# Row maxima of two heads negated and split before their transposition, and sent by one transfer instead of four

## The chip, the cores and the metric

The kernel runs on one core of one Trainium2 chip. Its metric is device microseconds of one execution. TensorE multiplies matrices and transposes, VectorE, ScalarE and GpSimd work on the elements, and the queue of SyncE (SP) issues every transfer between memories in program order.

## The reference, cut to what matters

The reference is a transformer block: a layer norm with a modulation, causal attention in 4 segments of 512 tokens with a memory carried from segment to segment, an output projection, and then a mixer MLP over the tokens. The attention of one head and one segment is what the change touches:

```python
# S=2048 tokens, D=1024, 32 heads of 32, N=4 segments of L=512
logits = einsum("bhqd,bhkd->bhqk", qs, ks) * scale + mask
p      = softmax(logits, axis=-1)
a_dot  = einsum("bhqk,bhkd->bhqd", p, vs)
num, den = phi(qs) @ M, phi(qs) @ z + 1e-6
o = g * num/den + (1-g) * a_dot
M, z = M + phi(ks)^T @ vs, z + sum(phi(ks))
```

The softmax needs the maximum of each row of logits, which is taken off before the exponential.

## The kernel before, in words

All matrices run as 32-bit numbers split in two parts, a high part and a rest (`split`), and products are made of three terms. The attention stage goes over 32 steps `t`: 8 groups of 4 heads, 4 segments, two passes. One step projects keys, values and queries of 4 heads (`project`, lines 194 and 202), and each of its 4 heads then goes through three stages that the loop at the end of the attention interleaves: `maxima` (three heads ahead), `scores`, and `values` (one head behind). Work that is prepared for later steps (weights, modulation rows, reloads) is planned between them. The program is written in this order, and a planner then orders the instructions of each engine by the times that it reckons; each engine runs its own list strictly in that order.

For each head there is a stacked tile `sk` with 98 rows: `stack` (lines 332 to 334) copies the parts of queries and keys into rows 0 to 95 by three transfers, with the queries in the left 512 columns and the keys in the right. Rows 96 and 97 hold, under the keys, ones, and under the queries the negated row maximum in two parts. So the product of `scores` over 98 rows gives logits less their maximum at once, already transposed for the product with the values. Before that product can run, rows 96 and 97 must have come.

`maxima` makes them. Four products on the 96 rows (line 438) give the logits with queries as rows, and VectorE reduces each to a column of `mx` (line 439). Every second head, TensorE transposes the 8 columns of two heads (line 445, `nmps`, in the one bank named `ms`), ScalarE writes the negated high part (line 447), VectorE the rest (line 448), and SP issues four transfers, one for each head and part, that bring them from 4 rows of 128 to one row of 512 (line 452). `scores` starts at line 473. There are 64 such pairs of heads.

The tiles `sk` exist twice, for even and odd steps, with one tile for each head:

```python
skt = [[q.tile([98, 2, L], F32R, name=f"sk{i}_{h}") for h in range(4)] for i, q in enumerate(sk_)]
```

The transfers use eight completion semaphores in turn; a transfer waits until the one eight places before it has landed.

Of the kernel before, what the change touches and what calls it, by code (L numbers as in the profile page):

```python
# [7 lines left out]
F32 = mybir.dt.float32  # L8
F32R = mybir.dt.float32r
F16 = mybir.dt.float16  # L10
BF16 = mybir.dt.bfloat16
AF = mybir.ActivationFunctionType
ALU = mybir.AluOpType
# [5 lines left out]
P = 128  # L19
NSEG, L = 4, 512  # L20
# [25 lines left out]
def attention_and_mlp(ctx, tc, x, wq, wkv, wo, beta, w1, b1, w2, b2, c, wm_a, wm_b, out):  # L46
    nc = tc.nc
    V, A, G, T, SY = nc.vector, nc.scalar, nc.gpsimd, nc.tensor, nc.sync
# [17 lines left out]
    a = par.__enter__()  # L66
# [9 lines left out]
    def bank(tag, bufs, name):  # L76
        return psum.tile([P, 512], F32, tag=tag, bufs=bufs, name=name)

    A.preload_act_table_set("natural_log_exp_and_others")
    ident = top.tile([P, P], F32, name="ident")  # L80
# [176 lines left out]
    for i in range(2):  # L257
        ps = bank("pj", 2, f"scps{i}")
# [43 lines left out]
    b = late.__enter__()  # L302
    skp = [tc.tile_pool(name=f"sk{i}", bufs=1, reuse_waits="tile") for i in range(2)]
    sk_ = [q.__enter__() for q in reversed(skp)]
    sk_.reverse()
    skt = [[q.tile([98, 2, L], F32R, name=f"sk{i}_{h}") for h in range(4)] for i, q in enumerate(sk_)]
    for sk in skt[0] + skt[1]:
        G.memset(sk[96:98, 1].bitcast(F32), 1.0)
    for g in range(NG):
        G.tensor_tensor(bdg[:, g, 0:128].rearrange("p (h e) -> p h e", h=4),  # L310
                        bd[:, 0:128].rearrange("p (h e) -> p h e", h=4),
# [10 lines left out]
    st = {}  # L322
# [3 lines left out]
    def stack(t, h):  # L326


        sk = st[t]["sk", h] = skt[t % 2][h]
        skf = sk.bitcast(F32)  # L330
        src = st[t]["sg"].bitcast(F32)[32 * h:32 * h + 32]
        SY.dma_start(skf[0:32], src[:, 0:3:2])
        SY.dma_start(skf[32:64], src[:, 0:4:3])
        last_sk[t, h] = SY.dma_start(skf[64:96], src[:, 1:3])

    def project(t, piece):
# [28 lines left out]
        elif piece == 2:  # L365
# [26 lines left out]
            for h in range(3):  # L392
                stack(t, h)
        else:
            stack(t, 3)
            vp, r1 = d["vp"], d["r1"]
            A.copy(vp[:, :, :, 33:65], r1)
# [28 lines left out]
                G.tensor_tensor(MZ[:, g], MZ[:, g], tm, op=ALU.add)  # L426

    def maxima(t, h):
        d = st[t]
        if h % 2 == 0:  # L430
            d["mx"] = b.tile([P, 2, 4], F32, tag="mx", bufs=2, name=f"mx{t}_{h}")
        mx = d["mx"]
        q, k = d["sk", h][0:96, 0], d["sk", h][0:96, 1]
        x = bank("s1", 2, f"sx_{t}_{h}")
        y = bank("s1", 2, f"sy_{t}_{h}")
        z = bank("s1", 2, f"sz_{t}_{h}")
        for i, o in ((0, x[:, 0:128]), (2, x[:, 128:512]), (1, y[:, 0:256]), (3, z)):
            T.matmul(o, q[:, 128 * i:128 * i + 128], k[:, 0:128 * i + 128], start=True, stop=True)  # L438
            marks[4 * t + h - LEADS, "V"] = V.tensor_tensor_reduce(  # L439
                o, o, mask[:, 384 - 128 * i:], 1.0, -3.0e38, op0=ALU.add, op1=ALU.max,  # L440
                accum_out=mx[:, h % 2, i:i + 1])
        if h % 2 == 0:
            return
        ps = bank("ms", 1, f"nmps{t}_{h}")
        T.transpose(ps[0:8, 0:128], mx.rearrange("p a b -> p (a b)"), ident)
        nt = [b.tile([8, P], F32R, tag=f"nt{i}", bufs=2, name=f"nt{i}_{t}_{h}") for i in range(2)]
        A.activation(nt[0], ps[0:8, 0:128], AF.Copy, scale=-1.0)
        V.scalar_tensor_tensor(nt[1], ps[0:8, 0:128], -1.0, nt[0].bitcast(F32), op0=ALU.mult, op1=ALU.subtract)
        for hh in range(2):
            sk = d["sk", h - 1 + hh]  # L450
            for part in range(2):
                SY.dma_start(sk[96 + part:97 + part, 0].bitcast(F32).rearrange("p (b n) -> p b n", n=128),
                             nt[part][4 * hh:4 * hh + 4].bitcast(F32))

    marks = {}

# [156 lines left out]
    for g in range(2, NG):  # L613
        n = 8 * g - 13
# [5 lines left out]
    for j in range(32):  # L620
        n = ML0 + MLS * j
        later(n, lambda j=j: mod_fetch(j), n + 2, lambda r, j=j: mod_late(j, r), "V")
    plan(WO0 - 3, lambda: spread(gaw, 0))
    for i in range(8):
        n = WO0 + WOS * i
        later(n, lambda i=i: wo_fetch(i), n + 2, lambda r, i=i: wo_split(i, r), "G")

    for n in range(-LEADS, 4 * NI + VL):
        at(scores, n)
        at(maxima, n + LEADS)  # L630
        at(values, n - VL)
        m = n + LEADP
        if 0 <= m + 4 < 4 * NI:
            t = (m + 4) // 4
            if its[t][:2] not in W:
                with tc.issue_after(last_sk[0, 3].ins):
                    load_w(its[t][1], its[t][0])
        if m >= 8:
            at(project, m)
        if 59 <= m < 67:  # L640
            seg, ct = 2 + (m - 59) // 4, 2 * ((m - 59) % 4)
            reload_h(seg, ct)
            reload_h(seg, ct + 1)
        if 4 * NI - 5 <= m < 4 * NI + 3:
            i = m - 4 * NI + 5
            for c in (2 * (i % 4), 2 * (i % 4) + 1):
                wop[c, i // 4] = new_page(f"wo{c}_{i // 4}")
                SY.dma_start(wop[c, i // 4].bitcast(F32), wos[c, i // 4])
        for f, engines in todo.pop(n, ()):
            with behind(n, engines):  # L650
                f()
# [270 lines left out]
    for u, (ph, g) in enumerate(units):  # L922
# [60 lines left out]
        t = tp.tile([P, 3, 512], F32, tag="tu", bufs=2, name=f"tu{g}")  # L983
# [66 lines left out]
```

## Time and profile before

| | us |
|---|---|
| median of 3 runs | 2264.99 (2263.22 to 2267.01) |
| profiled execution, its own time | 2269.23 |
| profiled execution, its span | 2267.5 |
| TensorE busy in the span | 2208.2 (97%) |
| VectorE busy | 1669.2 (74%) |
| ScalarE busy | 1147.0 (51%) |
| GpSimd busy | 752.3 (33%) |

The profile gives, for one execution, the busy time of each engine, groups of instructions by line and tile, who waited for whom, and the chain of work that ended last. Busy TensorE does not mean TensorE at its full rate, since matmuls overlap in the records. The granted clock of TensorE has a mean of 0.991 over the span.

### The profile page before, as it was taken

The numbers are of one execution on the slowest core, as the hardware profiler recorded it, in microseconds if no ns is written. First come the engines' busy times: TensorE is split into PE (matmuls) and PEld (weight loads), VectorE is DVE, ScalarE is ACT, GpSimd is POOL, SyncE is SP. The second block draws the span as 40 slices with busy tenths as digits, with TensorE's granted clock in tenths as the row PEclk, the third lists the DMA queues.
The fourth block names the chain that finished last, engine by engine and source line by source line (L and its number), as shares of the span: only waits on it lengthen the run. The fifth ranks groups of instructions, "written<-read, shape, count | busy, mean of one in ns | idle before, by whom it ended". The sixth has DMA issues, their size and how long they took to land.

```text
span 2267.5 us, 38381 instructions
## 1 busy us (share of the span) xinstructions
PE 2208.2 (97%) x13802; PEld 1902.5 (84%) x13802; DVE 1669.2 (74%) x3786; ACT 1147.0 (51%) x2090; POOL 752.3 (33%) x855
## 2 busy tenths in 40 slices
PE   7999999999999999999999999999999999999999
PEld 6888898888988889987888888888887888888887
DVE  6676676766776777655758866788889787868787
ACT  6476677665666656655536633533334242424232
POOL 5165565654666766654001200032332000000000
PEclk9999999999999999999999999999999999999999
DMA  6655565686567566683664587645558341414134
GB/s 260 203 171 170 148 193 160 194 265 222 161 192 213 167 184 199 177 251 125 216 222 167 204 311 287 249 177 228 209 204 298 143 153 56 153 56 144 56 121 149
DMA packets 174898, 423.06 MB, mean 187 GB/s; under 512 B 17492, under 2 KB 71796, under 8 KB 165748
## 3 DMA queue, kind: packets, MB, share of 16 engines
q1 hardware_dynamic: 174708, 420.61, 56.3%
q8 instruction: 110, 1.80, 0.3%
q14 instruction: 80, 0.66, 0.1%
HBM read 244.62 MB, written 125.06 MB: 163 GB/s over the span
## 4 chain that ended last, share of the span: by engine, by line
PE 84%; DVE 5%; DMA 4%; ACT 2%; POOL 2%; issue 2%; SPq 0%; DVEq 0%; ACTq 0%; POOLq 0%
PE mx L843 45%; PE nps L194 13%; PE qps L202 8%; PE po L723 6%; PE pv L502 3%; DMA sk<-nt 1%; PE sx L438 1%; PE a L473 1%; POOL ph L488 1%; PE sz L438 1%; PE rd L410 1%; PE a L476 1%; PE up L420 1%; DVE bU L124 1%; PE a L480 1%
## 5 line engine op out<-in xcount | busy, mean ns | idle before, releaser
L843 PE MATMUL mx<-bU,sp 128*128 128x512 f32 x2352 | 535.4, 389 | 3.1 <-DVE sp L124 1.9
L843 PEld LDWEIGHTS mx<-bU,sp 128*128 128x128 f32 x2352 | 440.9, 188 | 97.1 <-DVE sp L124 2.7
L194 PE MATMUL nps<-wv,h 128*128 128x256 f32 x3072 | 435.4, 283 | 4.0 <-POOL h L124 4.0
L121 ACT CAST sp<-wr 128x384 fp32r<-128x384 f32 (+2 forms) x408 | 217.3, 545 | 437.9 <-PE mx L843 366.0
L843 PE MATMUL mx<-bA,sp 128*128 128x512 f32 x1764 | 430.5, 389 | 0.0
L488 POOL TENSOR_TENSOR ph<-p,ph 128x640 f16<-128x640 f32 x256 | 377.6, 1496 | 153.0 <-ACT ph L486 152.9
L194 PEld LDWEIGHTS nps<-wv,h 128*128 128x128 f32 x3072 | 403.3, 190 | 10.9 <-POOL h L124 5.1
L843 PEld LDWEIGHTS mx<-bA,sp 128*128 128x128 f32 x1764 | 331.2, 188 | 68.7
L124 DVE TENSOR_TENSOR sp<-wr,sp 128x384 fp32r<-128x384 f32 (+2 forms) x408 | 261.6, 651 | 30.7 <-ACT sp L121 30.5
L850 DVE TENSOR_TENSOR ac<-mx,ac 128x512 f32<-128x512 f32 x280 | 189.3, 685 | 93.0 <-PE mx L843 90.5
L202 PE MATMUL qps<-h,wq 128*128 128x512 f32 x768 | 200.3, 406 | 2.3 <-DVE pv L505 1.1
L486 ACT CAST ph<-p 128x1280 f16<-128x1280 f32 x128 | 161.2, 1260 | 48.1 <-POOL p L484 47.5
L723 PE MATMUL po<-wo,ots 128*128 128x512 f32 x768 | 181.2, 392 | 1.9 <-DMA wo<-wos 1.2
L439 DVE CUSTOM_DVE_ANT_0 sx<-sx,mask 128x128 f32<-128x128 f32 (+1 forms) x256 | 109.9, 429 | 88.4 <-PE sx L438 87.2
L202 PEld LDWEIGHTS qps<-h,wq 128*128 128x128 f32 x768 | 144.3, 195 | 31.6 <-issue 2.8
L723 PEld LDWEIGHTS po<-wo,ots 128*128 128x128 f32 x768 | 142.8, 188 | 31.4 <-DMA wo<-wos 1.6
L484 POOL TENSOR_SCALAR_AFFINE_SELECT p<-p 128x256 f32<-128x256 f32 x256 | 121.0, 481 | 139.8 <-ACT p L477 69.6
L843 PE MATMUL mx<-bB,sp 128*128 128x512 f32 x588 | 164.0, 389 | 0.0
L502 PE MATMUL pv<-vp,ph 128*128 128x97 bf16 (+1 forms) x2560 | 144.7, 203 | 2.5 <-DVE red L509 1.3
L502 PEld LDWEIGHTS <-ph 128*128 128x128 f16 x2560 | 115.7, 99 | 26.4 <-issue 11.3
L843 PEld LDWEIGHTS mx<-bB,sp 128*128 128x128 f32 x588 | 110.4, 188 | 22.9
L850 DVE TENSOR_TENSOR cc<-mx,cc 128x512 f32<-128x512 f32 x140 | 94.7, 683 | 36.2 <-PE mx L843 36.1
(196 smaller groups left out, 3217.1 us busy)
## 6 DMA issues: line engine op xcount, KB each, us to landing
sk<-sg SPq DMA_DIRECT2D x384, 128.0 KB
wr<-in_w_dram SPq DMA_DIRECT2D x28, 1024.0 KB
wr<-in_w_dram SPq DMA_DIRECT2D x32, 768.0 KB
bstu<-ucd SPq DMA_DIRECT2D x28, 768.0 KB
wsp<-wv SPq DMA_DIRECT2D x32, 512.0 KB
rawm<-in_wm_b_dram SPq DMA_DIRECT2D x32, 512.0 KB
wv<-wsp SPq DMA_DIRECT2D x32, 512.0 KB
pcd<-cc SPq DMA_DIRECT2D x14, 1024.0 KB
```

What stands on the lines that cost most here:

```text
L121: A.copy(hi, src)
L124: lo_eng.tensor_tensor(lo, src, hi.bitcast(F32), op=ALU.subtract)
L194: T.matmul(ps[:, aa], h[:, j, 128 * tt:128 * tt + 128], wt[:, i, o:o + 256], start=(n == 0), stop=(n >= 6 * NK - 2), skip_group_check=True)
L202: T.matmul(ps, wt[:, i, o:o + 128], h[:, j], start=(k + n == 0), stop=(3 * k + n == 3 * NK - 1))
L439: marks[4 * t + h - LEADS, "V"] = V.tensor_tensor_reduce(o, o, mask[:, 384 - 128 * i:], 1.0, -3.0e38, op0=ALU.add, op1=ALU.max, accum_out= ...
L484: G.affine_select(w, w, pattern=[[0, 2], [1, 128]], compare_op=ALU.is_ge, fill=0.0, base=0, channel_multiplier=-1)
L486: marks[n, "A"] = A.copy(ph[:, 0], p32)
L488: marks[n, "G"] = G.tensor_tensor(ph[:, 1, c], p32[:, c], ph[:, 0, c], op=ALU.subtract)
L502: T.matmul(pv[:, i, 0:w], ph[:, part, o:o + 128], d["vp"][:, j, h, 0:w], start=(n == 0), stop=(n == 19), skip_group_check=True)
L723: T.matmul(ps, os_[:, i, P * ct:P * ct + P], wop[ct, nh][:, j], start=(n == 0), stop=(n == 3 * NK - 1))
L843: T.matmul(ps, ops[q][:, i, P * k:P * k + P], b[:, j], start=(m == 0 and first), stop=(m == 3 * nk - 1), skip_group_check=True)
L850: V.tensor_tensor(d, ps, d, op=ALU.add)
```

## The change

The four tiles of a step become one, `[98, 2, 2, 2, L]`: row, pair of heads, queries or keys, head within the pair, column. So the queries of the two heads of a pair lie beside each other, and rows 96 and 97 under them are one stretch of 1024 columns. `maxima` now makes both parts ahead of the transposition, on the 128x8 columns of maxima, with two VectorE instructions; TensorE transposes 16 columns instead of 8; ScalarE copies the 16x128 result; and one transfer brings it under the queries of both heads. The layout of `nt` (part, head, block) and of the two rows (head, block) agree. The third transfer of `stack`, whose target was one stretch of 1024 columns for each row, now has two stretches of 512.

```diff
-    skt = [[q.tile([98, 2, L], F32R, name=f"sk{i}_{h}") for h in range(4)] for i, q in enumerate(sk_)]
-    for sk in skt[0] + skt[1]:
-        G.memset(sk[96:98, 1].bitcast(F32), 1.0)
+    skt = [q.tile([98, 2, 2, 2, L], F32R, name=f"sk{i}") for i, q in enumerate(sk_)]
+    for sk in skt:
+        for h in range(2):
+            G.memset(sk[96:98, h, 1].bitcast(F32), 1.0)
...
-        sk = st[t]["sk", h] = skt[t % 2][h]
+        sk = st[t]["sk", h] = skt[t % 2][:, h // 2, :, h % 2]
...
+        neg = b.tile([P, 2, 8], F32R, tag="neg", bufs=2, name=f"neg{t}_{h}")
+        m8 = mx.rearrange("p a b -> p (a b)")
+        V.tensor_scalar_mul(neg[:, 0], m8, -1.0)
+        V.scalar_tensor_tensor(neg[:, 1], m8, -1.0, neg[:, 0].bitcast(F32), op0=ALU.mult, op1=ALU.subtract)
         ps = bank("ms", 1, f"nmps{t}_{h}")
-        T.transpose(ps[0:8, 0:128], mx.rearrange("p a b -> p (a b)"), ident)
-        nt = [b.tile([8, P], F32R, tag=f"nt{i}", bufs=2, name=f"nt{i}_{t}_{h}") for i in range(2)]
-        A.activation(nt[0], ps[0:8, 0:128], AF.Copy, scale=-1.0)
-        V.scalar_tensor_tensor(nt[1], ps[0:8, 0:128], -1.0, nt[0].bitcast(F32), op0=ALU.mult, op1=ALU.subtract)
-        for hh in range(2):
-            sk = d["sk", h - 1 + hh]
-            for part in range(2):
-                SY.dma_start(sk[96 + part:97 + part, 0].bitcast(F32).rearrange("p (b n) -> p b n", n=128),
-                             nt[part][4 * hh:4 * hh + 4].bitcast(F32))
+        T.transpose(ps[0:16, 0:128], neg.bitcast(F32).rearrange("p a b -> p (a b)"), ident)
+        nt = b.tile([16, P], F32R, tag="nt", bufs=2, name=f"nt_{t}_{h}")
+        A.copy(nt, ps[0:16, 0:128])
+        SY.dma_start(skt[t % 2][96:98, h // 2, 0].bitcast(F32).rearrange("p a n -> p (a n)"), nt.bitcast(F32))
```

## The prediction

> **What bounds the kernel now.** I read the page first: the head and part 1 for the engines, part 2 for the clock, part 4 for the chain that ended last.
>
> ```profile
> span 2267.5 us, 38381 instructions
> PE 2208.2 (97%) x13802; PEld 1902.5 (84%) x13802; DVE 1669.2 (74%) x3786; ACT 1147.0 (51%) x2090; POOL 752.3 (33%) x855
> PE 84%; DVE 5%; DMA 4%; ACT 2%; POOL 2%; issue 2%; SPq 0%; DVEq 0%; ACTq 0%; POOLq 0%
> PE mx L843 45%; PE nps L194 13%; PE qps L202 8%; PE po L723 6%; PE pv L502 3%; DMA sk<-nt 1%; PE sx L438 1%; PE a L473 1%; POOL ph L488 1%; PE sz L438 1%; PE rd L410 1%; PE a L476 1%; PE up L420 1%; DVE bU L124 1%; PE a L480 1%
> ```
>
> TensorE bounds it, and of the transfers one kind shows by name on the chain: `sk<-nt`, the one the change merges. It sits in the attention stage, which I cut into stretches by the view of windows (columns: window, length, then busy time and count of TensorE, its loads, VectorE, ScalarE and GpSimd, then granted clock, DMA share, GB/s):
>
> ```profile
> 75.00:565.00 490.00, 466.98 (x3918) 421.25 (x3917) 338.13 (x998) 325.87 (x613) 269.55 (x316) 0.96 0.64 190
> 565.00:1085.00 520.00, 508.99 (x4346) 458.03 (x4345) 352.15 (x1079) 315.58 (x550) 332.22 (x400) 1.00 0.61 184
> ```
>
> TensorE is idle for 23.0 us in the first stretch and 11.0 in the second, 34 together. That is the ceiling on removed stalls; beside it the first stretch runs at a mean clock of 0.96. VectorE is busy 69% in both, so it is late at places but is no bound. Next, the waits of TensorE alone (us in total, times, longest):
>
> ```profile
> PE a L473 <- DMA sk<-nt: 8.1, 7, 3.9
> PE sx L438 <- DVE mx L439: 5.6, 9, 1.8
> PE kps L370 <- DVE r L363: 3.3, 5, 1.5
> PE sx L438 <- DMA sk<-sg: 1.5, 2, 1.2
> PE nmps L445 <- DVE tm L425: 1.2, 2, 0.8
> PE nmps L445 <- DVE mx L439: 0.3, 1, 0.3
> ```
>
> The costliest wait of the stage is that of the scores for the rows of maxima: 7 of 64 pairs, 8.1 us. Nearly all else is waiting for VectorE. The transposition itself almost never waits for the maxima (0.3 us).
>
> **The change, part by part.** First the path from the transposition to the rows, from the views of the tiles `nt` and `nmps`, with min/median/max of each in ns:
>
> ```profile
> L452 SPq DMA_DIRECT2D sk<-nt x256: 572/573/1441, 98.3 to 1053.0; - x128
> L447 ACT ACTIVATE nt<-nmps x64: 247/261/268, 98.0 to 1050.8; 8x128 fp32r<-8x128 f32 x64
> L448 DVE SCALAR_TENSOR_TENSOR nt<-nmps,nt x64: 260/273/280, 99.5 to 1051.1; 8x128 fp32r<-8x128 f32 x64
> L445 PE MATMUL nmps<-ident,mx x64: 270/272/415, 96.7 to 1050.3; 128*8 128x128 f32 x64
> ```
>
> Before, the last row leaves after one ScalarE step, one VectorE step and four issues in a row: 0.261 + 0.273 + 4 x 0.573 = 2.83 us behind the transposition. After, it is 0.261 + 0.573 = 0.83 us, as a copy of 16 rows is taken at the price of 8 (the 128 columns set it; no row for 16). That is 2.0 us less for the last row. Ahead of the transposition come two VectorE steps on 128x8. The nearest row is that of `rdd`, of the same shape:
>
> ```profile
> L412 DVE TENSOR_SCALAR rdd<-rd x48: 147/161/174, 88.9 to 1001.8; 128x8 f32<-128x8 f32 x48
> ```
>
> Two of them are 0.32 us, so VectorE trades 64 x 0.273 = 17.5 us for 64 x 0.32 = 20.6 us: nothing, at 69% busy. The path from last maximum to landed rows shrinks by 2.0 - 0.32 = 1.7 us at least. It shrinks by more where issues did not follow each other at once, which the two largest stalls show. Here are SP's and TensorE's timelines (start, length, instructions, and in brackets the idle time before):
>
> ```profile
> 189.54 3.27 SPq L452 DMA_DIRECT2D sk<-nt  x4
> 524.28 4.37 SPq L452 DMA_DIRECT2D sk<-nt  x4
> ...
> 195.07 0.47 PE L473 MATMUL a<-sk 98*128 98x512 f32 x1 [2.08 <-DMA sk<-nt]
> 535.12 0.76 PE L473 MATMUL a<-sk 98*128 98x512 f32 x1 [3.93 <-DMA sk<-nt]
> ```
>
> There the four issues took 3.27 and 4.37 us; one would take 0.573, which is 2.7 and 3.8 less.
>
> *Stalls removed.* With 1.7 us taken off each wait: 1.7 of 3.93, 1.7 of 2.08, and the five others whole (8.1 - 3.93 - 2.08 = 2.1): 5.5 us. With the timelines' 2.7 and 3.8: all of the second, 3.8 of the first, 8.0 us. The landing at 535 stood behind a crowded machine (DMA share 0.93, in the row below), which an earlier issue does not cure. I take 6.5.
>
> *Clock.* These are the stretches around the two stalls; in the third place from the end is the granted clock:
>
> ```profile
> 190.00:195.50 5.50, 3.42 (x37) 2.82 (x35) 2.57 (x11) 4.82 (x10) 4.00 (x7) 1.00 0.76 243
> 195.50:202.30 6.80, 6.62 (x40) 5.54 (x39) 6.28 (x21) 3.21 (x7) 2.11 (x3) 0.50 0.52 196
> 527.00:533.40 6.40, 4.19 (x35) 3.94 (x33) 4.17 (x12) 0.46 (x2) 4.18 (x3) 1.00 0.93 329
> 533.40:540.20 6.80, 5.08 (x34) 4.63 (x35) 1.62 (x9) 1.16 (x2) 0.58 (x2) 0.50 0.66 149
> ```
>
> Right behind each of the two stalls TensorE ran 6.8 us at half clock. At full clock the first stretch's 6.62 us of work would take half: 3.3 us lost. The second loses 5.08 / 2 = 2.5 us. The first stall should go almost whole, so I count 3.3; the second stays in part, so I count nothing of its 2.5. Bounds: 0 to 5.8 us.
>
> [...]
>
> *Added wait.* TensorE's transposition now waits for the two VectorE steps, and behind it on TensorE's list stand the products of all other heads. Before, a late VectorE step at line 448 held only the transfers, and all but 7 of the scores came late enough not to notice. The trace has no such wait, so bounds: 0.3 us (the row of `nmps` for `mx`) below; above, the row of `kps`, 32 groups of transposes that wait for VectorE to free their bank, 3.3 us in 32, so 6.6 in 64. In the order of the program as built, the transposition now stands at least 27 matmuls behind the last logits of its pair, where it was 2, and 33 against 26 for the tenth of the pairs that is closest: the planner made room. I take 3.0, near the middle.
>
> *At nothing, with their cover.* SP issues 192 transfers fewer, 192 x 0.573 = 110 us of its queue; what TensorE can win by earlier stacks is the row `sx <- sk<-sg`, 0 to 1.5 us. The third transfer of each stack goes in two pieces:
>
> ```profile
> L332 SPq DMA_DIRECT2D sk<-sg x128: 585/606/1592, 57.5 to 999.4; - x128
> L334 SPq DMA_DIRECT2D sk<-sg x128: 560/592/1899, 58.4 to 1000.7; - x128
> ```
>
> Line 332 has such a form now; line 334 would go from 592 to 606 ns, 128 x 14 ns = 1.8 us on a queue that is relieved of 110.
>
> The bank `ms` is free one VectorE step sooner, which can win 0 to 1.2 us (`nmps <- tm`). Moving the tiles together adds no wait in the built program: the stacks and the products of a head wait for as many transfers as before.
>
> *Sum.* -6.5 - 3.3 + 3.0 = -6.8 us. On the profiled execution's own 2269.2 us (span 2267.5 and 1.7 around it) that is 2262.4. That execution lies 4.2 us above the median of the runs, 2265.0, and the forecast for the median is 2258.2. Some 0.2%, or 4.5 us, is what a measurement of this kernel can tell from no change.
>
> **The rivals.** *Slower: TensorE stands at the transposition.* VectorE's list is in order, and in the built program the second split is not right behind the last maximum: in 24 of 64 pairs at least three instructions that wait for another engine stand between. Each can be late, as the row of `pv` shows for all of VectorE:
>
> ```profile
> DVE pv L505 <- PE pv L502: 71.7, 57, 4.8
> ```
>
> If those 24 each cost TensorE what `kps` costs it, 3.3 / 5 = 0.66 us, this is 15.8 us against the 9.8 won: +6.0, 2271. It decides from 15 pairs on. For it speaks the row just shown, 1.26 us each time; against it, the room that the planner left. Chance 0.25.
>
> *No change: the stretches at half clock stay,* since they come from the mean business of TensorE and not from one stall, and only the stalls go: -6.5 + 3.0 = -3.5, 2261.5. [...] For it speaks that a third stretch of 6.8 us at half clock follows waits for VectorE and none for `nt`:
>
> ```profile
> 478.80:485.60 6.80, 6.02 (x33) 4.98 (x30) 6.44 (x21) 4.23 (x8) 4.35 (x6) 0.50 1.02 334
> ...
> 478.06 0.95 PE L502 MATMUL pv<-vp,ph 128*128 128x97 bf16 x20 [1.28 <-DVE red L509]
> ```
>
> Against it: both great stalls have one right behind them. The same result, about 2262 to 2267, follows if the new order of the engines' lists deals out other stalls, some 26 us of which (34 - 8.1) the change doesn't aim at. Chance 0.2.
>
> *More than forecast,* both stalls and both stretches gone and no new wait: -8.0 - 5.8 - 1.5 - 1.2 = -16.5, 2248.5. This asks that the landing at 535 moves by as much as its issue, against the DMA share of 0.93. Chance 0.1.
>
> **How the numbers follow.** Forecast 2258.2 with chance 0.45, its own range 2252 to 2260.5. With the last rival, faster by over 0.2% has 0.55; the second rival is the 0.2 within; the first is the 0.25 slower. The range reaches from the far end of the gains, 2249, to just over the slower case, 2272.
>
> **What would show it.** Right: in the waits of TensorE, `a <- sk<-nt` falls from 8.1 to under 2 us; no half clock behind a wait for `nt`; SP's issues of `nt` fall from 256 to 64 at some 0.6 us; `nmps` waits under 4 us in all for VectorE; idle time between 75 and 1085 falls from 34 to some 30 us or less. Wrong: `nmps <- DVE neg` of 10 us or more, or a landing of the merged transfer that is as late as the fourth was.

## The result and the profile after

The changed kernel is slower: 2278.73 us (six runs, 2277.09 to 2287.58) against 2264.1 (six runs, 2261.72 to 2267.2). The ratio is 1.0059, 95% interval 1.0043 to 1.0075, or some 15 us. The time lies above the range of the prediction.

The profiled execution after (its own time 2279.11 us). The head, part 1 and the first line of the chain:

```profile
span 2277.3 us, 38100 instructions
PE 2211.5 (97%) x13802; PEld 1905.9 (84%) x13802; DVE 1690.4 (74%) x3850; ACT 1144.9 (50%) x2090; POOL 753.5 (33%) x851
PE 81%; DVE 7%; POOL 3%; ACT 3%; DMA 3%; issue 2%; SPq 0%; ACTq 0%; POOLq 0%; DVEq 0%
```

VectorE is busier by 21 us, where 3 were forecast, and on the chain VectorE and GpSimd have grown while the transfers have shrunk. The two windows of the attention stage:

```profile
75.00:565.00 490.00, 465.47 (x3941) 420.39 (x3940) 346.15 (x1030) 326.38 (x614) 271.35 (x318) 0.97 0.65 192
565.00:1085.00 520.00, 503.58 (x4279) 453.31 (x4279) 361.71 (x1104) 310.13 (x544) 330.63 (x397) 0.99 0.60 180
```

TensorE is idle for 24.5 + 16.4 = 41 us instead of 34: 7 of the 9.8 us by which the two spans differ. In these windows VectorE is busy 707.9 us; before it was 690.3. What TensorE waits for, cut to rows of the attention stage:

```profile
PE sx L441 <- DVE mx L442: 6.7, 11, 2.2
PE kps L371 <- DVE r L364: 5.7, 5, 2.4
PE sx L441 <- DMA sk<-sg: 4.1, 2, 2.3
...
PE pv L504 <- POOL ph L490: 3.6, 4, 1.4
PE pv L504 <- DVE red L511: 3.3, 5, 1.2
PE a L475 <- DMA sk<-nt: 3.2, 3, 1.9
...
PE nmps L452 <- DVE neg L450: 0.5, 1, 0.5
```

One profile of a kernel is not enough to read single waits. A second one of the same changed kernel, taken with the last experiments below, has these rows:

```profile
PE a L475 <- DMA sk<-nt: 6.9, 4, 2.5
...
PE kps L371 <- DVE r L364: 5.7, 5, 2.4
...
PE pv L504 <- DVE red L511: 3.7, 5, 1.2
...
PE sx L441 <- DMA sk<-sg: 2.3, 1, 2.3
```

The wait that the change aims at has fallen from 8.1 us to 3.2 in the one and to 6.9 in the other. In both the transposition waits only 0.5 us for the new steps, and in both two waits for VectorE elsewhere have grown: `kps <- r` from 3.3 to 5.7 us, and `pv <- red`, which was this before:

```profile
PE pv L502 <- DVE red L509: 1.3, 1, 1.3
```

The rest of TensorE's 7 us of new idle time lies now here, now there: `sx <- mx`, `pv <- ph` and `sk<-sg` have grown clearly in the first profile alone. The group view shows what the two new steps cost:

```profile
L449 DVE TENSOR_SCALAR neg<-mx 128x8 fp32r<-128x8 f32 x64 | 36.0, 562 | 0.3
L450 DVE SCALAR_TENSOR_TENSOR neg<-mx,neg 128x8 fp32r<-128x8 f32 x64 | 25.3, 395 | 0.8
```

That is 61.3 us of VectorE, three times the 20.6 forecast, for 17.5 removed. The views of the tiles `neg` and `nt` (min/median/max in ns) show that the price isn't one price:

```profile
L449 DVE TENSOR_SCALAR neg<-mx x64: 154/365/1383, 88.0 to 1052.3; 128x8 fp32r<-128x8 f32 x64
L450 DVE SCALAR_TENSOR_TENSOR neg<-mx,neg x64: 149/168/1384, 88.5 to 1053.0; 128x8 fp32r<-128x8 f32 x64
...
L454 ACT CAST nt<-nmps x64: 236/248/256, 98.1 to 1056.8; 16x128 fp32r<-16x128 f32 x64
L455 SPq DMA_DIRECT2D sk<-nt x64: 617/660/1354, 98.3 to 1057.1; - x64
```

The same instruction takes 0.15 or 1.38 us. The timelines of VectorE and of GpSimd in one stretch show what decides it:

```profile
303.84 1.12 DVE L449 TENSOR_SCALAR neg<-mx 128x8 fp32r<-128x8 f32 x1
304.99 1.31 DVE L450 SCALAR_TENSOR_TENSOR neg<-mx,neg 128x8 fp32r<-128x8 f32 x1
...
303.52 2.77 POOL L490 TENSOR_TENSOR ph<-p,ph 128x640 f16<-128x640 f32 x2 [1.37 <-ACT ph L488]
306.24 0.41 POOL L486 TENSOR_SCALAR_AFFINE_SELECT p<-p 128x256 f32<-128x256 f32 x1
```

GpSimd runs two steps of line 490, which the row takes together, from 303.52 to 306.29; half of their 2.77 us is over at 304.9. The first new step of VectorE lasts until 304.96, the second until 306.30. Over all 64 pairs, counted in the trace: 44 of the first steps start while a GpSimd step runs; they sum to 32.7 us and end 0.03 us (median) after it. The other 20 take 154 to 173 ns. So the trace shows these steps waiting inside their own duration, where no view of waits has it.

Their 43.8 us more than the step removed are not all new work for VectorE, whose total grew by 21.2. Other steps that work on SBUF became shorter, such as these two groups (995 and 1014 ns before; 16 of the 32 and 15 of the 16 started while a GpSimd step ran, now 12 and 9):

```profile
L399 DVE TENSOR_TENSOR vp<-r,vp 128x512 bf16<-128x512 f32 x32 | 26.5, 829 | 0.9 <-ACT vp L398 0.9
...
L602 DVE TENSOR_TENSOR wor<-wor,woh 128x512 fp32r<-128x512 f32 x16 | 11.5, 728 | 0.1
```

That is 10 us of it: part of the waiting for GpSimd seems only to have moved to the new steps.

### The profile page after: what moved, and what is told of

Read it like the earlier page. It is cut to its first block, busy times and chain, and to the rows that moved or that the text cites. A ratio compares the mean times of both kernels' runs of the same rounds, so it can differ in the third digit from the quotient of the medians.

```text
span 2277.3 us, 38100 instructions
## 1 busy us (share of the span) xinstructions
PE 2211.5 (97%) x13802; PEld 1905.9 (84%) x13802; DVE 1690.4 (74%) x3850; ACT 1144.9 (50%) x2090; POOL 753.5 (33%) x851
## 4 chain that ended last, share of the span: by engine, by line
PE 81%; DVE 7%; POOL 3%; ACT 3%; DMA 3%; issue 2%; SPq 0%; ACTq 0%; POOLq 0%; DVEq 0%
PE mx L845 45%; PE nps L194 11%; PE qps L202 7%; PE po L725 7%; PE pv L504 3%; POOL ph L490 2%; PE a L475 1%; PE sx L441 1%; ACT ph L488 1%; PE sz L441 1%; PE a L478 1%; PE rd L411 1%; PE up L421 1%; DVE wv L124 1%; PE a L482 1%
## 5 line engine op out<-in xcount | busy, mean ns | idle before, releaser
L476 ACT ACTIVATE p<-a,shift 128x512 f32<-128x512 f32 x128 | 88.2, 689 | 68.8 <-PE a L475 46.7
```

## The experiments

Each kernel ran beside the kernel before on the same chip; ratios are to that, with 95% intervals. I theorised first that the two steps hold up VectorE, by waiting for GpSimd; rivals were the layout, the new place in the lists of the engines, and the single transfer.

**The layout alone.** One tile instead of four, the third transfer of the stacks in two pieces; the split behind the transposition and the four transfers stay.

```diff
...
-        sk = st[t]["sk", h] = skt[t % 2][h]
+        sk = st[t]["sk", h] = skt[t % 2][:, h // 2, :, h % 2]
```

> Only the tiles move: four heads of a step in one tile, the split behind the transposition and the four transfers as before. Theory 'port' (the two new VectorE steps on 128x8 wait for GpSimd's instruction and hold up VectorE's list): no VectorE step is added, so within 4.5 us of before. Rival 'layout' (the merged tile, its third stack transfer in two pieces): most of the 14.6 us shows here, 2275 or more. Rival 'order' (any new list of the engines costs some us by chance): anywhere within 10 us of before, up or down.

Measured: 2265.29 against 2266.61, 1.0002 [0.9992, 1.0012]. The layout costs nothing.

**The split ahead alone.** The old tiles and four transfers; the two VectorE steps of the change.

```diff
+        V.tensor_scalar_mul(neg[:, 0], m8, -1.0)
+        V.scalar_tensor_tensor(neg[:, 1], m8, -1.0, neg[:, 0].bitcast(F32), op0=ALU.mult, op1=ALU.subtract)
...
-        V.scalar_tensor_tensor(nt[1], ps[0:8, 0:128], -1.0, nt[0].bitcast(F32), op0=ALU.mult, op1=ALU.subtract)
...
+        A.copy(nt, ps[0:16, 0:128])
```

> Only the split moves: negated and split by VectorE on 128x8 ahead of the transposition, separate tiles and four transfers for each pair as before. 'Port': the two steps take some 0.4 to 0.55 us on average where they take 0.16 without GpSimd, VectorE is busy some 40 us longer, and the kernel is slower than before by 10 to 20 us, at least as slow as the changed kernel, which has the shorter transfer to set against it. 'Layout': within 4.5 us of before. 'Order': no telling, within 10 us.

Measured: 2276.57, 1.004 [1.0027, 1.0054]. Two groups of this kernel:

```profile
L446 DVE TENSOR_SCALAR neg<-mx 128x8 fp32r<-128x8 f32 x64 | 34.9, 546 | 0.4
L447 DVE SCALAR_TENSOR_TENSOR neg<-mx,neg 128x8 fp32r<-128x8 f32 x64 | 28.7, 448 | 0.7
```

The steps cost as much as in the changed kernel (63.6 us), and most of the loss is here without the single transfer.

**The pair added to the kernel before,** its result used by nobody.

> The kernel before, with the two VectorE steps on 128x8 added ahead of each transposition and their result used by nothing. 'Port': steps of 0.4 to 0.55 us on average that end with GpSimd's instruction; 5 to 15 us slower than before though no path leads through them, since VectorE's list stands meanwhile. A rival of the path (it is the transposition's wait for them that costs): no slower than the next kernel, within 4.5 us of before.

Measured: 2274.61, 1.0037 [1.0024, 1.0049]. Nothing waits for these steps' result, so a loss needs no wait at the transposition.

**Two reductions instead of the pair,** likewise unused. They have the same shape, but all 128 of them took 0.10 to 0.16 us, in a stage in which GpSimd was busy for 595 of 1010 us.

```diff
+        V.tensor_reduce(neg[:, 0], m8.unsqueeze(2), axis=AX.X, op=ALU.add)
+        V.tensor_reduce(neg[:, 1], neg[:, 0].unsqueeze(2), axis=AX.X, op=ALU.add)
```

> The control of the kernel with the unused pair: instead of these, two unused VectorE reductions on 128x8, which read one operand from SBUF. 'Port': each takes 0.2 us or less whatever GpSimd does; under 5 us slower than before, and the difference to the unused pair is what the waiting costs. 'Order': as far from before as the unused pair, up or down.

Measured: 2284.45, 1.0082 [1.0068, 1.0096]. This was a miss: the cheaper control came out slower than the pair. The planner had written other lists for the two kernels, so that each of the comparisons so far is of two things at once. From here on some kernels have the order of every engine's instructions fixed to a given list, by order alone, with no waits added. "In before's lists" means: what both kernels have stands as in the kernel before.

**The changed work in before's lists, and before's work in the changed kernel's.**

> The changed kernel's work in the order of before: each engine's list is that of the kernel before, instruction for instruction; the two VectorE steps stand right behind the pair's last maximum, the one transfer where the first of the four stood, line 448's step is gone. Theory 'order' (the 14.6 us come from the new lists that the planner made, not from the new steps): gone, 2254 to 2268, faster than before if the forecast's removed stalls were right. Rival 'port' (the VectorE steps wait for GpSimd and hold up VectorE): still slower than before by 7 us or more, 2273 and up.

> The reverse: the work of the kernel before (split behind the transposition, four transfers, separate tiles) in the lists of the changed kernel; only line 448's VectorE step is left to the planner, and the four transfers stand where the one stood. 'Order': slower than before by 10 us or more, 2275 to 2285. 'Port': within 4.5 us of before.

Measured: 2284.12, 1.0081 [1.0068, 1.0094], and 2308.73, 1.0191 [1.0174, 1.0209]. The second lies above both of its expectations. Lists fit the work they were made for; the wrong ones cost 42 us there, so a list by itself isn't good or bad. The first case shows that the planner's new order does not make the loss by itself: without it the change loses more. Its waits and groups:

```profile
PE sx L442 <- DVE mx L443: 11.8, 14, 2.3
...
PE nmps L453 <- DVE neg L451: 6.8, 6, 2.0
...
L451 DVE SCALAR_TENSOR_TENSOR neg<-mx,neg 128x8 fp32r<-128x8 f32 x64 | 34.9, 546 | 2.2
L450 DVE TENSOR_SCALAR neg<-mx 128x8 fp32r<-128x8 f32 x64 | 24.7, 386 | 2.2
```

**The unused pair and the unused reductions, both in before's lists.** This is the control that missed above, with the lists held.

> Before with the unused VectorE pair on 128x8 (as in the kernel with the extra pair), but in the lists of before, the pair right behind the last maximum. This is the price of the two steps alone. 'Order': under 4 us, as VectorE is idle three tenths of the stage. 'Port': the 8 us that the extra pair cost stay, 2272 and up.

> Before with the two unused reductions, in the lists of before, at the same places. 'Order': the 18 us that they cost vanish, within 4 us of before. 'Port': also near before, as each takes 0.15 us; then the difference to the pair at the same places is the price of the waiting for GpSimd, 40 us of VectorE's time in all, of which the end sees 3 to 8.

Measured: 2296.11, 1.0131 [1.0111, 1.0151], and 2278.46, 1.0054 [1.0039, 1.007]. The groups of the second:

```profile
L448 DVE TENSOR_REDUCE neg<-neg 128x8 f32<-128x8 f32 x64 | 10.3, 161 | 2.2
L447 DVE TENSOR_REDUCE neg<-mx 128x8 f32<-128x8 f32 x64 | 10.3, 161 | 2.2
```

So 20.6 us of added work on a VectorE that is 69% busy cost 12 us at the end, where at most 4 were expected; and waiting for GpSimd, in the same places, cost another 18, where 3 to 8 were expected.

**Fewer transfers alone.** The split stays behind the transposition; in the merged tile one transfer for each part, two instead of four, first in before's lists and then as the planner orders it. The cut is against the kernel before.

```diff
-        for hh in range(2):
-            sk = d["sk", h - 1 + hh]
-            for part in range(2):
-                SY.dma_start(sk[96 + part:97 + part, 0].bitcast(F32).rearrange("p (b n) -> p b n", n=128),
-                             nt[part][4 * hh:4 * hh + 4].bitcast(F32))
+        for part in range(2):
+            SY.dma_start(skt[t % 2][96 + part:97 + part, h // 2, 0].bitcast(F32).rearrange(
+                "p a (b n) -> p (a b) n", n=128), nt[part].bitcast(F32))
```

> Merged tile, the split behind the transposition as before, and two transfers for each pair (one for each part, both heads in one row) instead of four, in the lists of the kernel before. No step is added to VectorE. If shorter issues are worth what the forecast said and only the VectorE steps spoiled it: 3 to 8 us faster, 2258 to 2263. If the issues were hidden anyway: within 4.5 us of before.

> The same with the lists that the planner makes for it. If lists in themselves cost or win by chance: anywhere within 15 us of before. If the list follows the work well: as fast as in the lists of before or faster, 2255 to 2264.

Measured: 2267.07, 1.0 [0.9988, 1.0012], and 2264.35, 0.9996 [0.9985, 1.0007]. Taking 128 issues of some 0.6 us off SP's queue gives no time that can be seen; the wait of the scores for `sk<-nt` was 9.8 and 7.1 us in the two profiles.

**The split ahead, off VectorE.** The changed kernel, with ScalarE writing the negated maxima twice (rounded and whole) and GpSimd taking the difference.

```diff
-        V.tensor_scalar_mul(neg[:, 0], m8, -1.0)
-        V.scalar_tensor_tensor(neg[:, 1], m8, -1.0, neg[:, 0].bitcast(F32), op0=ALU.mult, op1=ALU.subtract)
...
+        A.activation(neg[:, 0], m8, AF.Copy, scale=-1.0)
+        A.activation(n8, m8, AF.Copy, scale=-1.0)
+        G.tensor_tensor(neg[:, 1], n8, neg[:, 0].bitcast(F32), op=ALU.subtract)
```

> The changed kernel with the split ahead taken off VectorE: ScalarE writes the negated maxima twice (rounded and whole), GpSimd subtracts; one transfer; new lists by the planner. VectorE is then relieved by 17.5 us against before. 'VectorE's time counts though it is 69% busy': faster than before by 5 us or more, and faster than the changed kernel by 15 or more. 'The list is what counts': no telling, within 15 us of before.

> The same work in the lists of the kernel before; only the three new steps on ScalarE and GpSimd are left to the planner. 'VectorE's time counts': 18 us for the changed work in these lists turn into nothing or a gain, 2255 to 2268. Rival: the transposition waits for GpSimd, whose steps on ph take 1.5 us each, in a third of 64 pairs for 0.7 us: 14 us slower than before.

Measured: 2260.85, 0.9974 [0.9963, 0.9985] as the planner orders it, and 2289.46, 1.0107 [1.0094, 1.012] in before's lists. In the second TensorE stands at the transposition, which is the slower rival's mechanism, with GpSimd in VectorE's place:

```profile
PE nmps L455 <- POOL neg L453: 29.7, 17, 3.9
```

**The price of the two steps inside the change.** The pair is replaced by two reductions of the same shape, in the changed kernel's own lists and in before's. `zer` is a tile of zeros: these kernels leave out the rounding and the low part.

```diff
+        V.tensor_reduce(neg[:, 0].bitcast(F32), m8.unsqueeze(2), axis=AX.X, op=ALU.add, negate=True)
+        V.tensor_reduce(neg[:, 1].bitcast(F32), zer.unsqueeze(2), axis=AX.X, op=ALU.add)
```

> The changed kernel in its own lists, with the pair of VectorE steps replaced by two reductions on 128x8 at the same places, which don't wait for GpSimd. The first negates the maxima unrounded, the second only writes zeros: the rounding and the low part are left out of the computation. What the changed kernel loses by the waiting alone: if that is its whole loss, 2255 to 2266; if VectorE's two steps cost by their own 0.3 us a pair and by the list, 2270 or more. From the lists of before (30 us for the pair, 12 for the reductions) I expect 10 to 18 us off the changed kernel, 2261 to 2268.

> The same work in the lists of the kernel before, steps right behind the last maximum; the rounding and the low part are left out again. Against the changed work in these lists (18 us over before) the difference is the waiting; if it is worth the 18 us that it was for the unused pair, this is at 2266, and the transfer and the split ahead give nothing between them.

> The kernel with the split on ScalarE and GpSimd once more, beside the changed kernel on one chip: 3 to 8 us faster than before and 15 to 20 faster than the changed kernel, if the first look was no accident of a chip.

> The changed kernel on the same chip as the three above: 12 to 17 us slower than before.

Measured, on one chip: 2270.81, 1.002 [1.0009, 1.003]; 2263.34, 0.9991 [0.998, 1.0001]; off VectorE 2258.07, 0.9966 [0.9954, 0.9978]; the changed kernel 2277.37, 1.0059 [1.0046, 1.0072]. The reductions in before's lists, groups and waits:

```profile
L452 DVE TENSOR_REDUCE neg<-mx 128x8 f32<-128x8 f32 x64 | 10.3, 161 | 2.2
L453 DVE TENSOR_REDUCE neg<-zer 128x8 f32<-128x8 f32 x64 | 9.7, 151 | 0.0
...
PE sx L444 <- DMA sk<-sg: 5.7, 4, 2.9
PE sx L444 <- DVE mx L445: 5.1, 9, 1.1
...
PE a L478 <- DMA sk<-nt: 3.0, 4, 1.6
```

With steps that cost what I had forecast, and with nothing else in the lists moved, the change is no change that can be told: what `sk<-nt` gives up, 8.1 to 3.0 us, comes back in good part as `sx <- sk<-sg`, 1.5 to 5.7, in this one profile of each. With the real steps the same lists gave 2284.1, or 1.0081, on another chip. So waiting for GpSimd is worth 0.0090 of the time there, 20 us; in the lists that the planner made for the change it is 7 us (2277.37 less 2270.81). Those lists cushion the long steps, and cost 7.5 us (2270.81 less 2263.34) where the steps are short. The second reduction does not depend on the first, as the second split does; what that is worth is counted with the waiting. It should be little, since the unused reductions above, where the second does depend on the first, took 161 ns each.

On this chip the changed kernel loses 10.9 us against before (12 to 17 were expected). 6.6 of them go when the steps don't wait; the other 4.3 stay in these lists with short steps too, where I had expected none (2261 to 2268), and are gone in before's lists. So the waiting is shown as the larger part of the loss in the planner's lists and as all of it in before's.

The version off VectorE, in the planner's lists, beats both kernels: 0.34% below before and 19 us below the changed kernel on the same chip. Its GpSimd and ScalarE groups, the windows and the waits:

```profile
L452 POOL TENSOR_TENSOR neg<-n,neg 128x8 fp32r<-128x8 f32 x64 | 20.9, 327 | 35.6 <-ACT n L451 34.6 <-ACT mb L709 0.9
L450 ACT ACTIVATE neg<-mx 128x8 fp32r<-128x8 f32 x64 | 13.8, 216 | 11.9 <-DVE mx L442 11.3 <-DVE rdd L413 0.5
...
75.00:565.00 490.00, 471.11 (x4077) 428.62 (x4076) 343.24 (x1002) 343.49 (x696) 288.33 (x364) 0.99 0.66 197
565.00:1085.00 520.00, 508.25 (x4245) 455.29 (x4244) 336.25 (x1025) 311.83 (x602) 330.37 (x416) 1.00 0.60 181
...
PE sx L441 <- DVE mx L442: 4.6, 5, 1.7
...
PE pv L506 <- DVE red L513: 3.9, 5, 1.1
...
PE up L421 <- DVE am L415: 3.5, 3, 2.1
...
PE a L477 <- DMA sk<-nt: 1.8, 3, 1.1
PE sx L441 <- DMA sk<-sg: 1.6, 2, 1.3
```

VectorE's busy time in the two windows is 679.5 us, 28 below the changed kernel. Part of what `sk<-nt` gives up is paid back here too (`pv <- red` 3.9 us, 1.3 before, and `up <- am` 3.5, which had no wait before), yet TensorE's idle time falls from 34 to 30.6 us. How much of the gain is the relief of VectorE and how much the new lists is not separated: in before's lists the same work is slower than before.

## Why the prediction was wrong, point by point

**The price of the two new steps: the step that failed.** "Two of them are 0.32 us" took the duration of `rdd` (161 ns) because its shape is the same. The new steps do take 0.15 to 0.17 us when no GpSimd step runs; those that start while one runs wait for its end, the first of the two for 44 of 64 pairs, the second for 30. `rdd` does not: in before 29 of its 48 start while a GpSimd step runs, and none takes more than 0.174 us. It reads PSUM, and the new steps read only SBUF; but that alone does not decide it, as the reciprocal behind `rdd` (line 413) reads only SBUF too, on the same 128x8, and takes at most 0.205 us, with 36 of 48 started while a GpSimd step runs. Summed, the new steps took 61.3 us instead of 20.6. The waiting is worth 6.6 us of the loss in the planner's lists and 20 in before's. The trace of before had the sign of it, in steps of one size that read only SBUF. In the first two groups 16 of 32 and 15 of 16 start while a GpSimd step runs, and take 1.43 and 0.87 us (medians); the others of the first group take 0.63 to 0.69 us. In the third, behind the attention, no GpSimd step runs beside them:

```profile
L398 DVE TENSOR_TENSOR vp<-r,vp 128x512 bf16<-128x512 f32 x32 | 31.8, 995 | 2.1 <-ACT vp L397 2.1
...
L600 DVE TENSOR_TENSOR wor<-wor,woh 128x512 fp32r<-128x512 f32 x16 | 16.2, 1014 | 0.4 <-ACT woh L599 0.3
...
L124 DVE TENSOR_TENSOR bA<-h,bA 128x512 fp32r<-128x512 f32 x12 | 8.0, 684 | 0.0
```

In the changed kernel the splits that start while a GpSimd step runs end 0.02 to 0.03 us after it (medians), and the reductions of the same shape in their place take 0.10 to 0.16 us. Why the ones wait and the others don't, no run shows.

**"Nothing, at 69% busy": failed too.** 20.6 us of cheap steps, added with all lists held, cost 12 us in the kernel before. That VectorE's list is in order and TensorE reads its results all through the stage, so that a busy share of 69% left no cover, is how I explain it; no run shows that reason by itself.

**Stalls removed, 6.5 of 8.1: the wait falls, the gain doesn't come.** The wait is 3.2 and 6.9 us in the two profiles of the changed kernel; under 2 was forecast. Over all profiles of this case it is 6.4 to 9.9 us in the ten with two or four transfers for a pair, and 1.4 to 4.4 in the six others with one, so that the fall is real but its size for this kernel is open. The stacks' wait, which was put at a gain of 0 to 1.5, was not smaller: 4.1 and 2.3 us, and 5.7 in before's lists. With the extra VectorE work at the forecast's price the sum is then 0.9991, a gain of 2 us whose interval reaches no change, where -6.8 was forecast.

**Clock, -3.3: not there.** The stall for `nt` at 195 is gone, and the clock falls at the same place all the same. These are the windows around it in the changed kernel (third from the end: granted clock):

```profile
190.40:196.20 5.80, 3.67 (x33) 2.56 (x32) 5.80 (x17) 3.81 (x9) 3.65 (x3) 0.91 0.20 75
196.20:203.00 6.80, 6.80 (x21) 5.68 (x22) 5.86 (x18) 5.76 (x11) 4.42 (x5) 0.57 0.38 142
```

Ahead of it TensorE now waits for VectorE, 1.04 us at most at a time. Between 75 and 1085 us the clock falls 8 times before and 9 times after, and both profiles have 37.5 us at half clock there, in stretches of 3.4 and 6.8 us. In the 3.4 us ahead of each of these falls, as long as the shorter stretches, TensorE was busy for 0.7 to 2.7 us, and its longest idle time was 0.3 to 2.4 us. So the half clock did not hang on the one stall; in that the rival was right. Its reason, that the half clock comes from how busy TensorE is, is not shown: in before TensorE was busy for 1.64 us between 1028.8 and 1032.2, and the clock stayed at 1.00 there and in the 12.8 us behind. Over all runs of the two kernels the mean clock fell from 0.992 to 0.9905, which over 2265 us is an estimated 3 us lost.

**Added wait at the transposition, +3.0: too high.** It is 0.5 us. The planner's room held, and in before's lists, without that room, it is 6.8. So the sign of being wrong that I had named, 10 us or more of `nmps <- DVE neg`, did not show, though the prediction was wrong: the loss came by another way.

**At nothing.** The layout and the third stack transfer were right (1.0002). SP's issues are right in number and nearly in price (64 of 0.66 us, taken as 0.573), and ScalarE's copy of 16 rows took 0.248 us, where 0.261, the time for 8, was taken. SP's relief was worth nothing that can be seen, as the two transfers show for 128 of the 192 issues.

**The rivals.** The slower rival had the right sign and engine: VectorE's list in order, and a late second split. Its place was wrong, since TensorE does not stand at the transposition but at later transposes and products that wait for VectorE (`kps <- r`, `pv <- red`). Its 2271 fell short because it set 9.8 us of gains against the loss. Its 15.8 us of loss lie near the 14.6 measured, but by luck: they price 24 late transpositions, which did not come. What stays open is how much of the loss another planning would save: no list made with the true, varying durations was run.

## What to carry to other kernels

Take a new instruction's duration from a row with the same operation, the same shape and the same places of its operands: here a VectorE split on 128x8 lasted up to 1.38 us, until the GpSimd step beside it ended, while a reduction of that shape took 0.16 us at most; and ScalarE with GpSimd was the better place for the split, in lists made for that (2258.07 against 2277.37 us). VectorE, busy 69%, was not free here: 20.6 us more of it cost 12. When a planner orders the instructions, a control must hold the lists fixed, or it measures the lists. And read a single wait from more than one profile: the same kernel gave 3.2 and 6.9 us for one wait.

## What the runs showed of the hardware that was not expected

A 128x8 step of VectorE took up to 1.38 us, nine times its 0.15, with no wait shown anywhere: the waiting is counted as busy time. So VectorE's busy share in this kernel holds waiting; of the 61.3 us of the two new steps it is an estimated 41, as 128 steps of 0.16 us would be 20.5.

The granted clock went with the time lost, by and large. The mean clock over a kernel's runs was 0.985 for the slowest kernel (2309 us), 0.987 for the unused pair in before's lists (2296), 0.9905 changed (2277), 0.992 before (2266.5) and 0.996 for the best (2258). The order is not strict: the kernel off VectorE in before's lists had 0.990 at 2289 us, as the unused pair had at 2275. From before to the best it is 0.0035, by an estimate 8 us of 2266, beside a gain of 8.4; in the windows TensorE's idle time fell only from 34 to 30.6 us. That fewer stalls raise the clock is argued from these kernels; no run changed the clock alone.
